# Two state updates placed earlier in an attention pipeline, and one shift of the routing moved to ScalarE

## The chip, the core and the metric

The kernel runs on one core of a Trainium2 chip. The time is the device time of one execution in microseconds (us). The engines that matter are TensorE (PE in the profile; its weight loads are PEld), VectorE (DVE), ScalarE (ACT), GpSimd (POOL) and SyncE (SP), which issues most transfers.

## What is computed

Two blocks follow each other. The first is a linear attention with a decaying state, for 4 batches, 8 heads, 768 tokens and a head width of 48; the second sends each token through one of 8 experts.

```python
for t in range(S):                       # attention, for each b, h
    cur = einsum('bhd,bhe->bhde', u * kt, vt)
    y[:, :, t] = einsum('bhd,bhde->bhe', rt, state + cur)
    state = w * state + einsum('bhd,bhe->bhde', kt, vt)
...
x = y as (B, S, H * D)                   # 4 x 768 x 384
fresh_e = argmax(x @ w_gate)             # 8 experts
e = fresh_e if s == 0 or sigmoid(x @ w_local) < 0.5 else prev_e
out = softmax(x @ w_gate)[e] * (relu(x @ w1[e]) @ w2[e])
```

The expert of a token is thus its own best one, or the one that the token before it had: a running choice along each sequence. w1 is 384x1024 for each expert, w2 1024x384.

## The kernel before

**The items.** The attention is worked off in 16 items, n = 0 to 15: a batch n // 4 and a pair of heads n % 4. Each item has 768 tokens, in 6 chunks (c) of 128. The partitions hold two heads of 48 each, at 0 and at 64. For each item the class runs these steps, each a method:

- `load`: three transfers on SP's queue: rk (r and k with the head's rows on the partitions), kv (k and v with the tokens on the partitions) and vT.
- `scale`: six products on POOL, all with both inputs in SBUF: rw, r times powers of the decay (L229, two halves); ke, k times the decay to the end of its chunk (L212, two halves); pd, r times k (L216, two halves). Up to item 2 the order is pd, ke (with rw on VectorE), for item 4 ke, rw, pd, for the others rw, ke, pd. These products lie in buffers that serve in turn.
- `keys`: kw on VectorE (L236), k divided by the powers of the decay.
- `added`: ten matmuls on PE (L248; the profile shows each matmul of the items as two rows, or passes, each transpose as one), one for each of 5 chunks and 2 heads: what each chunk adds to the state. They write `T`, 240 columns of the PSUM tile mp. There is one T for all items.
- `states`: one scan on VectorE (L254) that reads T and writes S, the state ahead of each chunk.
- `own`: four matmuls on PE (L264) on pd and one product with vT on VectorE (L268): each token's own term. It opens the PSUM tile y.
- `scores(n, half)`: twelve matmuls (L283) on kw and rw for three chunks, into one of two PSUM tiles that serve in turn ("pair"). It returns the masking product on VectorE (am, L285), which the caller places.
- `inside`: the products of am with v (L292), 24 PE passes for an item, added into y.
- `before`: the products of S with rw (L305), added into y, then ACT's copy of y to xT (L309).
- `turn`: six transposes (L318) into a "pair" tile and ACT's copies to x (L320); with a batch's last item, x goes to DRAM.

With a whole batch done, `logits` (L331) multiplies xT by the gate weights and `token_logits` turns the result, so that VectorE has each token's 9 logits.

**The order.** Each engine works through its own instructions in the order in which `run` (L341 to L479) issues them; a semaphore wait stops the engine and all that is queued behind. Iteration n of the loop holds, for most n: turn(n-2), added(n), states(n), scale(n+1), inside(n-1), before(n-1), scores(n+1) with the first half's mask at once and the second half's mask kept (`keep`), own(n), keys(n+2), keep(). Up to n = 2 the item's own added and states close the iteration. At n = 3 the scores are those of item 3 itself (`ahead`, L438), and the order behind them is own(3), added(3), keep(), states(3). At n = 4 the scores of 4 and of 5 follow each other.

**The routing in between.** E is 8 experts. The tokens' experts are found in two groups of two batches each. The steps of the first group are laid into iterations 9 to 15 of the attention (g is 8):

- n = 9 (g+1): `experts_of`: VectorE finds each token's largest logit (L671), compares (L672), weights (L673) and, in a second part at the iteration's end, forms a key (L675 to L678).
- n = 10 (g+2): behind own(10), `router.keys` turns the keys on PE into the tile mp (L684), columns that T partly shares, and `router.runs` makes the running maximum on VectorE (L689).
- n = 11 (g+3): `turn_runs` turns it back on PE (L694) into columns of mp beyond T, `last` (L701) spreads the last column, and `one_hot` (L707 to L714) yields each token's expert `ei[:, 1]` and its one-hot form oh (L712). L714, the last of it, shifts the expert number left by 9 as an integer: the number times 512, the base of the expert's slots.
- n = 12 (g+4): `counts` (L721, L722) and `ranks` (L728 to L737). n = 13: `slots`, whose L774 adds the shifted number to a token's rank. n = 14, 15: `columns`, `numbers`, `places`.

The second group does the same once, after the attention (from about 112 us), among the experts' first matmuls. From there to the end, PE works through the experts' layers.

mp is one PSUM tile of 512 columns for T, the turned keys, the turned runs and, in the first iterations, the powers of the decay (written by L157 and its like, for items 0 to 3). What writes it waits until what was there has been read.

Of the kernel before, what the change touches and what calls it, by code (L numbers as in the profile page):

```python
# [11 lines left out]
F32 = mybir.dt.float32  # L12
I32 = mybir.dt.int32
Act = mybir.ActivationFunctionType
Alu = mybir.AluOpType
# [5 lines left out]
P = 128  # L21
# [5 lines left out]
E, F = 8, 1024  # L27
# [5 lines left out]
ST = 4  # L33
# [22 lines left out]
def spread(ap, axis, n):  # L56

    a = ap.unsqueeze(axis)
    return a.to_broadcast([n if i == axis else s for i, s in enumerate(a.shape)])


class Attention:
# [278 lines left out]
    def run(self, router, fetch, heads):  # L341


        def pair(name):
            t = self.banks(name)
            return [t[:, 0], t[:, 1]]

        M = B * HP

        mp, mp_end = router.mp, 2 * P + 2 + (NCH - 1) * DH  # L350

        g = GROUPS[0][1] * HP
        for n in range(M + 1):
            if n + AHEAD - 1 < M:
                self.load(n + AHEAD - 1)
            elif n + 2 == M:
                fetch()
            if n == 0:
                self.scale(0)
                self.keys(0)  # L360
                self.tables()
                self.scores(0, 0)()
                self.scores(0, 1)()
                self.own(0)
                self.nc.scalar.copy(self.first, self.tab[:, 1, 0])
                self.turn_ends(slice(1, HP))
                self.warm(3)
                self.added(0)
                self.reciprocals(1)
                self.states(0)  # L370
                self.scale(1)
                continue
            if n < 3:

                self.keys(n)
                self.inside(n - 1)
                self.before(n - 1)
                if n == 2:
                    self.turn(0, pair("tp"))
                self.nc.scalar.copy(self.first, self.tab[:, n + 1, 0])  # L380
                self.scores(n, 0)()
                keep = self.scores(n, 1)
                self.own(n)
                keep()
                self.added(n)
                self.states(n)
                if n == 1:
                    self.reciprocals(2)
                self.scale(n + 1)
                continue  # L390
            if n < M:
                self.turn(n - 2, pair("tp"))
                if n == 3:
                    self.reciprocals(3)
                if n < 5:
                    self.keys(n)
                if n > 3:
                    self.added(n)
                    self.states(n)
            if n == 4:  # L400
                self.keys(5)
            if n > HP and n % HP == 1:
                self.token_logits(n // HP - 1, pair("lq")[0])
            if n == g + 1:
                router.experts_of(0, (0,))
            if n == g + 5:
                router.slots(0)
                router.columns(0)
            if n == g + 6:
                router.numbers(0)  # L410
            if n == M:
                router.shares(0)
            if n + 1 < M:
                self.scale(n + 1)
            if 3 <= n < 6:
                router.constants(n - 3)
            if n == M:
                self.turn(M - 2, pair("tp"))
            self.inside(n - 1)
            if n == g + 3:  # L420

                router.turn_runs(0, mp[:, mp_end:])
            self.before(n - 1)
            if n == 6:
                router.cast()
            if n == M:
                break
            if n == g + 3:
                router.last(0, mp[:, mp_end:])
                router.one_hot(0, (0,))  # L430
            if n == g + 7:

                router.summed(0, 0)
                router.copied(0, self.nc.vector.tensor_copy)
                router.head(pair("tb")[0])
                heads()

            ahead = n if n < 5 else n + 1  # L438
            if ahead < M:
                self.scores(ahead, 0)()  # L440
                keep = self.scores(ahead, 1)
            if n % HP == 0:

                keep()
                self.own(n)
                self.logits(n // HP - 1, pair("lp")[0])
                if n == 4:
                    self.scores(5, 0)()
                    self.scores(5, 1)()
                    self.keys(6)  # L450
                if n == g + 4:
                    router.counts(0, [mp, mp[:, E * NC // 2:]])
                    router.ranks(0, (0,))
                if n > 4:
                    self.keys(n + 2)
                if n == g + 4:
                    router.ranks(0, (1,))
            else:
                self.own(n)
                if n == g + 2:  # L460
                    router.keys(0, mp)
                    router.runs(0)
                if n == 3:
                    self.added(3)
                if 4 < n < M - 2:
                    self.keys(n + 2)
                if ahead < M:
                    keep()
                if n == 3:
                    self.states(3)  # L470
            if n == g + 1:
                router.experts_of(0, (1,))
            if n == g + 3:
                router.one_hot(0, (1,))
            if n == g + 5:
                router.places(0, 0)
            if n == g + 6:
                router.places(0, 1)
        self.inner.close()  # L479
# [81 lines left out]
class Router:  # L561
# [27 lines left out]
    def open(self, i, pool):  # L589
        g, c = self.g[i], self.g[i]["nc"]  # L590
        for name, shape, dt in (
                ("mx", [P, c], F32), ("eq", [P, c, E], F32), ("k", [P, c], F32), ("key", [P, c], F32),
                ("run", [c, P], F32), ("rn", [P, c], F32), ("inc", [P, c + 1], F32),
                ("ei", [P, 3, c], I32), ("oh", [P, E, c], F32),
                ("exc", [P, E, c + 1], F32), ("pos", [P, E, c], F32), ("far", [P, EARLY, c], F32),
                ("r", [P, c], F32), ("si", [P, 3, c], I32),
                ("eqv", [P, c, E * ST], F32), ("val", [P, c, E * ST], F32), ("ohq", [P, c, P], F32),
                ("ex", [P, c, E], F32), ("sm", [P, c], F32), ("pe", [P, c], F32)):
            if name != "far" or i == 0:
                g[name] = pool.tile(shape, dt, name=f"{name}{i}")  # L600
# [102 lines left out]
    def one_hot(self, i, parts=(0, 1)):  # L703

        nc, g = self.nc, self.g[i]
        if 0 in parts:
            nc.vector.memset(g["inc"][:, 0:1], 0.0)  # L707
            nc.vector.tensor_tensor_scan(g["inc"][:, 1:], g["bc"], self.go, 0.0, Alu.max, Alu.mult)
            nc.vector.tensor_tensor(g["ei"][:, 0], g["inc"][:, :g["nc"]], g["rn"], op=Alu.max)
            nc.vector.tensor_scalar(g["ei"][:, 1], g["ei"][:, 0], E - 1, None, Alu.bitwise_and)  # L710
        if 1 in parts:
            nc.vector.tensor_tensor(g["oh"], spread(g["ei"][:, 1], 1, E), spread(self.ie, 2, g["nc"]), op=Alu.is_equal)  # L712

            nc.vector.tensor_scalar(g["ei"][:, 2], g["ei"][:, 1], 9, None, Alu.arith_shift_left)  # L714

    def counts(self, i, bank):

# [52 lines left out]
    def slots(self, i):  # L770

        nc, g = self.nc, self.g[i]
        nc.vector.tensor_reduce(g["r"], g["pos"].rearrange("p e c -> p c e"), axis=AX.X, op=Alu.add)
        nc.vector.scalar_tensor_tensor(g["si"][:, 0], g["r"], float(ST * P - 1), g["ei"][:, 2], Alu.min, Alu.add)  # L774
        nc.vector.tensor_scalar(g["si"][:, 1], g["si"][:, 0], P - 1, None, Alu.bitwise_and)
        nc.vector.tensor_scalar(g["si"][:, 2], g["si"][:, 0], 7, None, Alu.arith_shift_right)

# [34 lines left out]
    def heads(self, table, out):  # L812
        self.nc.vector.tensor_reduce(out, table[:, :EARLY, :2], axis=AX.X, op=Alu.add)
# [80 lines left out]
def route(tc, once, ps, lt, ident, gates):  # L894
# [57 lines left out]
    nc.vector.tensor_copy(ccol, cp[:NC, :1])  # L952
    run = tl("run", [NC, P])
    nc.vector.tensor_tensor_scan(run, rows, rows, ccol, Alu.max, Alu.max)
    rp = bank("rp")
    nc.tensor.transpose(rp[:, :NC], run, ident[:NC, :NC])
    ei = tl("ei", [P, NC], I32)
    nc.vector.tensor_copy(ei, rp[:, :NC])
# [756 lines left out]
```

## Time and profile before

| | |
|---|---|
| time, median of 3 runs | 384.11 us (383.83 to 384.48) |
| time of the profiled execution | 385.54 us |
| its span in the trace | 383.8 us |
| granted TensorE clock | 0.996 |
| PE busy | 366.4 us, 95% of the span |
| PEld busy | 322.5 us, 84% |
| DVE busy | 251.6 us, 66% |
| POOL busy | 150.7 us, 39% |
| ACT busy | 106.5 us, 28% |

The span runs from the first to the last recorded instruction; the time of the same execution is 1.7 us longer. The shares are means over the whole span; the kernel has stages with different limits, and the attention ends at about 112 us, so the shares of its stretches have to be read by themselves:

| stretch, us | length | PE | DVE | POOL | DMA share |
|---|---|---|---|---|---|
| 0 to 27 | 27 | 24.01 | 21.68 | 20.56 | 0.93 |
| 27 to 36 | 9 | 7.33 | 6.84 | 8.60 | 1.02 |
| 36 to 66 | 30 | 29.59 | 23.47 | 30.00 | 0.98 |
| 66 to 80 | 14 | 12.49 | 12.87 | 12.59 | 1.00 |
| 80 to 112 | 32 | 29.18 | 24.91 | 15.07 | 0.51 |
| 112 to 384 | 272 | 263.79 | 161.78 | 63.83 | 0.41 |

Each number under an engine is its busy time in us in that stretch. A line of the timeline below gives the start, the length, the engine, the source line, the operation and its output and inputs with their sizes; "x20" means 20 instructions of the same kind in one row, and a square bracket at the end the idle time ahead and what ended it.

### The profile page before, as it was taken

Reading aid. Unit: us, or ns where it says so; the run is one execution under the profiler, and the core shown is the slowest. Engines: PE = TensorE matmul, PEld = TensorE weight load, DVE = VectorE, ACT = ScalarE, POOL = GpSimd, SP = SyncE. Lnnn points to the kernel's source line nnn. Section 1 sums busy time; section 2 is a strip of 40 time slices with the busy share of each in tenths; the row PEclk is TensorE's granted clock in tenths of the full one; section 3 lists DMA queues with packets and bytes.
Section 4 is the critical chain, followed back from the end, with each engine's and each line's share of the span. In section 5 each row is a group of like instructions: output and inputs, shape, how many; then the busy total and the mean of one; then the engine's idle time right before and its main releaser. Section 6 shows DMA issues by size and latency. Waiting matters only on the chain. (4 is left out here: it accounts for less than half of the span.)

```text
span 383.8 us, 9675 instructions
## 1 busy us (share of the span) xinstructions
PE 366.4 (95%) x3846; PEld 322.5 (84%) x3846; DVE 251.6 (66%) x722; ACT 106.5 (28%) x288; POOL 150.7 (39%) x212
## 2 busy tenths in 40 slices
PE   7998999898999999999999999999999999999992
PEld 6775777676759998999999999999989899899971
DVE  6888778978935745587556757658758758456400
ACT  4131232222222111322323233234234233232220
POOL 8689999877222041411432313213313113012022
PEclk9999999999999999999999999999999999999998
DMA  7999998989115880830561165145246146064011
GB/s 255 410 411 409 407 387 305 372 303 393 55 32 200 321 351 13 288 151 23 205 205 64 42 189 209 54 172 206 76 165 227 38 172 233 10 213 171 3 37 36
DMA packets 17478, 74.97 MB, mean 195 GB/s; under 512 B 2730, under 2 KB 6587, under 8 KB 14865
## 3 DMA queue, kind: packets, MB, share of 16 engines
q1 hardware_dynamic: 10048, 56.89, 39.4%
q0 software_dynamic: 3424, 9.52, 7.6%
q10 hardware_dynamic: 3952, 7.87, 5.6%
q8 instruction: 32, 0.52, 0.6%
q14 instruction: 22, 0.17, 0.1%
HBM read 64.83 MB, written 9.51 MB: 194 GB/s over the span
## 5 line engine op out<-in xcount | busy, mean ns | idle before, releaser
L1272 POOL DMA_INDIRECT out_dram<-yo,sid x27 | 26.7, 988 | 102.4 <-ACT yo L1267 79.0
L1123 PE MATMUL h<-exT,w1t 128*128 128x168 f32 (+4 forms) x240 | 54.9, 327 | 0.0
L1127 DVE TENSOR_TENSOR hT<-h,hs 128x168 f32<-128x168 f32 (+3 forms) x60 | 21.0, 351 | 46.6 <-PE h L1123 31.0
L1046 POOL DMA_INDIRECT xg<-x_d,gid x29 | 31.2, 1075 | 37.7 <-DVE sm L881 17.4
L1123 PEld LDWEIGHTS h<-exT,w1t 128*128 128x128 f32 x240 | 41.7, 190 | 0.3 <-issue 0.3
L1073 PE MATMUL h<-exT,w1t 128*128 128x192 f32 (+1 forms) x192 | 38.3, 338 | 0.0
L1192 PE MATMUL y<-factors,sums 128*128 128x192 f32 x168 | 36.8, 326 | 0.0
L1123 PE MATMUL h<-xs,ws 128*128 128x168 f32 (+4 forms) x144 | 35.2, 326 | 0.0
L216 POOL TENSOR_TENSOR pd<-rk 128x384 f32<-128x384 f32 x32 | 31.4, 1003 | 9.3 <-PE y L264 7.1
L285 DVE TENSOR_TENSOR am<-pair,kept 128x768 f32<-128x768 f32 x32 | 30.0, 950 | 7.2 <-PE pair L283 6.6
L1073 PEld LDWEIGHTS h<-exT,w1t 128*128 128x128 f32 x192 | 32.3, 190 | 1.5 <-issue 0.2
L1123 PEld LDWEIGHTS h<-xs,ws 128*128 128x128 f32 x144 | 25.5, 190 | 4.3 <-ACT hs L1130 1.2
L1192 PEld LDWEIGHTS y<-factors,sums 128*128 128x128 f32 x168 | 28.9, 190 | 0.0
L292 PE MATMUL y<-am,kv 128*64 128x128 f32 x384 | 25.1, 276 | 1.1 <-DVE y L268 1.1
L212 POOL TENSOR_TENSOR ke<-kv,endT 128x288 f32<-128x288 f32 x32 | 24.9, 799 | 2.5 <-DMA kv<-in_kv_dram 1.7
L283 PE MATMUL pair<-rw,kw 48*64 48x128 f32 (+1 forms) x768 | 22.9, 249 | 1.4 <-ACT end L167 0.6
L229 POOL TENSOR_TENSOR rw<-rk,tab 128x384 f32<-128x384 f32 x26 | 23.7, 930 | 1.2 <-DMA rk<-in_rk_dram 1.2
L309 ACT COPY xT<-y 128x768 f32<-128x768 f32 (+1 forms) x16 | 12.5, 780 | 40.0 <-PE y L305 40.0
L292 PEld LDWEIGHTS y<-am,kv 128*64 128x64 f32 x384 | 21.1, 137 | 2.6 <-DVE y L268 1.6
L1192 PE MATMUL y<-w2t,hT 128*128 128x192 f32 x96 | 23.0, 328 | 0.0
L1060 DVE COPY exT<-tp 128x384 f32<-128x384 f32 (+6 forms) x29 | 14.0, 488 | 13.8 <-PE tp L1059 13.6
L283 PEld LDWEIGHTS pair<-rw,kw 48*64 48x64 f32 x768 | 19.4, 133 | 3.7 <-issue 1.8
(279 smaller groups left out, 732.8 us busy)
## 6 DMA issues: line engine op xcount, KB each, us to landing
w1t<-in_w_dram SPq DMA_DIRECT2D x9, 1536.0 KB, 6.7
w2t<-in_w_dram SPq DMA_DIRECT2D x9, 1536.0 KB, 7.6
rk<-in_rk_dram SPq DMA_DIRECT2D x15, 768.0 KB, 9.2
kv<-in_kv_dram SPq DMA_DIRECT2D x16, 584.0 KB, 6.9
vT<-in_vT_dram SPq DMA_DIRECT2D x16, 384.0 KB, 10.0
x_d<-x ACTq DMA_DIRECT2D x4, 1152.0 KB, 10.3
w1t<-in_w_dram ACTq DMA_DIRECT2D x1, 1536.0 KB
w2t<-in_w_dram ACTq DMA_DIRECT2D x1, 1536.0 KB
```

The lines of the kernel that those rows point to most:

```text
L212: nc.gpsimd.tensor_mul(t["ke"][:, p::2], t["k"][:, p::2], spread(self.endT[:, p, hp], 1, C2))
L216: nc.gpsimd.tensor_mul(t["pd"][:, z], t["rT"][:, z], t["kT"][:, z])
L229: engine.tensor_mul(t["rw"][:, z], t["rT"][:, z], spread(pw, 1, z.stop - z.start))
L283: nc.tensor.matmul(sc[f * DP:(f + 1) * DP, h, i, x:], lhsT=t["kw"][q, c, o * DP:(o + 1) * DP], rhs=t["rw"][q, c, x:], start=True, stop=True)
L285: return lambda: nc.vector.tensor_mul(t["am"][:, g], sc, spread(self.kept[:, g:g + 3], 1, 2))
L292: nc.tensor.matmul(t["y"][p * DP:(p + 1) * DP, h, c2 * P:(c2 + 1) * P], lhsT=t["v"][:, (2 * c + h) * DH:(2 * c + h) * DH + DP], rhs=t["am" ...
L1046: self.nc.gpsimd.indirect_dma_start(out=xg[:n], out_offset=None, in_=self.x_d[:rows], in_offset=bass.IndirectOffsetOnAxis(ap=u["gid"][:n, ...
L1073: nc.tensor.matmul(h[:, :n], lhsT=u["w1"][:, m, kk, :], rhs=u["xT"][:, kk, :], start=(kk == 0), stop=(kk == DK - 1))
L1123: nc.tensor.matmul(out, lhsT=a, rhs=b, start=start and k == 0, stop=stop and k == len(terms) - 1, skip_group_check=True)
L1127: nc.vector.tensor_tensor(out, a, b, op=Alu.add)
L1192: return lambda: nc.tensor.matmul(bank[:, x * half:(x + 1) * half], lhsT=a, rhs=b, start=(j == 0 and x == 0), stop=(j == FK // 2 - 1), ski ...
L1272: self.nc.gpsimd.indirect_dma_start(out=out.rearrange("n (h d) -> (n h) d", h=2) if half else out, out_offset=bass.IndirectOffsetOnAxis(ap ...
```

## The change

It has three parts.

A. At n = 3, added(3) and states(3) are issued ahead of scores(3). Before, added(3) stood behind own(3), and states(3) behind the second mask.

B. added(11) is issued in iteration 10, between own(10) and `router.keys`. Before, it stood at the start of iteration 11, behind turn(9). states(11) stays where it was.

C. The shift L714 leaves VectorE. In its place ACT writes the expert number times 512 as a float into a tile of its own, eb, with one ACTIVATE (Copy, scale 512). L774 reads eb. This holds for both groups, so it concerns two instructions in all.

```diff
@@ run
                 if n > 3:
-                    self.added(n)
+                    if n != g + 3:
+                        self.added(n)
                     self.states(n)
...
             ahead = n if n < 5 else n + 1
+            if n == 3:
+                self.added(3)
+                self.states(3)
             if ahead < M:
                 self.scores(ahead, 0)()
                 keep = self.scores(ahead, 1)
...
                 self.own(n)
                 if n == g + 2:
+                    self.added(n + 1)
                     router.keys(0, mp)
                     router.runs(0)
-                if n == 3:
-                    self.added(3)
                 if 4 < n < M - 2:
                     self.keys(n + 2)
                 if ahead < M:
                     keep()
-                if n == 3:
-                    self.states(3)
@@ open
-                ("ei", [P, 3, c], I32), ("oh", [P, E, c], F32),
+                ("ei", [P, 2, c], I32), ("eb", [P, c], F32), ("oh", [P, E, c], F32),
@@ one_hot
             nc.vector.tensor_tensor(g["oh"], spread(g["ei"][:, 1], 1, E), spread(self.ie, 2, g["nc"]), op=Alu.is_equal)
-            nc.vector.tensor_scalar(g["ei"][:, 2], g["ei"][:, 1], 9, None, Alu.arith_shift_left)
+            nc.scalar.activation(g["eb"], g["ei"][:, 1], Act.Copy, scale=float(ST * P))
@@ slots
-        nc.vector.scalar_tensor_tensor(g["si"][:, 0], g["r"], float(ST * P - 1), g["ei"][:, 2], Alu.min, Alu.add)
+        nc.vector.scalar_tensor_tensor(g["si"][:, 0], g["r"], float(ST * P - 1), g["eb"], Alu.min, Alu.add)
```

The order in which the engines receive their instructions changes as the diff says and nowhere else: PE has the same matmuls, with a row of ten moved in two places, VectorE has one scan moved and two instructions fewer, ACT has two more, POOL and SP have the same in the same order.

## The prediction, made before the changed kernel was run

> Items are counted from 0, as in the code: the title's items 4 and 12 are n = 3 and n = 11. "am(4,0)" is the masked score of item 4's first half (L285).
>
> **What bounds the kernel now.** The chain of waits ends in an output DMA and says nothing of the middle, so I read the windows by stage first: in 36 to 66 us PE is busy 29.59 of 30 us, after 112 us 263.79 of 272. But in 27 to 36 us it is busy 7.33 of 9, in 66 to 80 12.49 of 14. PE is the bound with two leaks, and the change sits in both. POOL (30.00 of 30) and the DMA (share 0.98) are full in 36 to 66 too, so each must be shown not to be the next bound. Then the timeline of the first leak:
>
> ```profile
> 28.37 0.96 DVE L285 TENSOR_TENSOR am<-pair,kept 128x768 f32<-128x768 f32 x1 [0.84 <-PE pair L283]
> 29.34 0.66 PE L248 MATMUL mp<-kv,ke 128*48 128x48 f32 x20
> 29.92 0.80 PE L318 MATMUL pair<-ident,xT 112*128 112x112 f32 x6
> 30.39 0.95 DVE L285 TENSOR_TENSOR am<-pair,kept 128x768 f32<-128x768 f32 x1
> 31.26 0.64 DVE L254 TENSOR_TENSOR_SCAN S<-step,mp 128x240 f32<-128x240 f32 x1
> 32.00 0.66 PE L248 MATMUL mp<-kv,ke 128*48 128x48 f32 x20 [1.28 <-issue]
> 32.46 1.53 PE L292 MATMUL y<-am,kv 128*64 128x128 f32 x24
> 33.91 0.79 PE L305 MATMUL y<-rw,S 48*48 48x128 f32 x18
> ```
>
> [...]PE idles 1.28 us before added(4) at 32.00. The page calls it "issue", but scan(3), which still reads T, ends at 31.90, and added(4) overwrites T: that is the wait. Second leak:
>
> ```profile
> 65.98 2.40 DVE L672 TENSOR_TENSOR eq<-lt,mx 128x96 f32<-128x96 f32 x1
> 66.71 1.55 POOL L212 TENSOR_TENSOR ke<-kv,endT 128x288 f32<-128x288 f32 x2
> 69.40 1.97 POOL L216 TENSOR_TENSOR pd<-rk 128x384 f32<-128x384 f32 x2 [1.14 <-PE y L264]
> 69.60 0.79 PE L318 MATMUL pair<-ident,xT 112*128 112x112 f32 x6 [0.37 <-DVE am L285]
> 75.56 0.79 PE L318 MATMUL pair<-ident,xT 112*128 112x112 f32 x6 [0.45 <-DVE am L285]
> 76.79 0.66 PE L248 MATMUL mp<-kv,ke 128*48 128x48 f32 x20 [0.44 <-issue]
> 78.33 0.63 DVE L254 TENSOR_TENSOR_SCAN S<-step,mp 128x240 f32<-128x240 f32 x1
> 79.02 0.23 PE L694 MATMUL mp<-ident,run 12*128 12x12 f32 x1 [0.25 <-DVE inc L707]
> 85.86 0.98 DVE L714 TENSOR_SCALAR ei<-ei 128x12 int32<-128x12 int32 x1
> 88.30 1.50 PE L331 MATMUL pair<-xT,wp 128*32 128x384 f32 x16 [0.31 <-DVE am L285]
> ```
>
> From 65.30 to 79 DVE runs without a gap, and PE waits for it at 69.60, 75.56 and 79.02. The wait at 76.79 is for the run scan L689 (76.29, 0.40 long), which reads the same tile mp.
>
> [...]L714 takes 978 ns beside POOL's L229 and 167 ns later, when POOL is idle; L672 2399 against 258 ns. Inputs from PSUM (L285, L268, L236, L254) show no such stretch. [...]Seven VectorE instructions met that here: L676, L677, L712, L714, L729, L737 got through at the end of the POOL instruction then running; L672 let two such ends pass (66.74, 67.50) and finished only when POOL stopped at 68.26 because pd(11) waited for own(9). [...]the trace's ACT CAST L662 of 128x8 took 200 ns. The built order adds no table load.
>
> **Part A, item 3.** No work is added or removed; 20 passes (0.66 us) and a scan (0.64 us) move. Added(3) goes behind before(2), whose last weights are loaded by 26.92 (L305 at 26.24, 0.68 long). Its inputs are there: ke(3) since 24.82, the last write of mp before it (L157) at 26.39. It issues to 27.45 and ends at about 27.58. PE idled then anyway: 0.39 us until kw(3) at 27.50, so scores(3), queued behind it, starts as before. Cover gone: 0.1 us at most. Scan(3) runs 27.65 to 28.30 in VectorE's 0.84 us gap before am(3,0) at 28.37. Then:
> - PE: turn(2) follows own(3), at 29.40 (am(3,0) must end, 29.33), not 29.92. Added(4) needs scan(3) (28.30) and ke(4) (28.95): 29.98, not 32.00.
> - Inside(3) then needs L268(3) (ends 30.49) for its first 10 passes and am(3,1) (ends 31.34) for the other 14. What is late next is am(3,1). From 31.40, 14 passes at 0.85 us (the same 14 at 18.39) end at 32.25; with the usual 0.17 us before(3) starts at 32.42, not 33.91: 1.49 us earlier.
> - VectorE: kw(4) from 31.26, scan(4), kw(5) to 33.64; am(4,0) is wanted at 33.82. It holds by 0.2 us.
>
> Is it kept? POOL has no gap from 27.40 to 68.26, so its times don't move; PE's margins to it are own(4) 3.0 us (35.80 against pd(4) 32.79), scores(5) 3.2, scores(6) 3.1, scores(7) 3.4, scores(8) 3.2, scores(9) 3.4. All exceed 1.5. Loads: rk(6), issued at 23.05 and at most 11 us in flight, lands by 34.4 and is wanted at 39; the gap grows afterwards. So A brings **-1.5 us** by iteration 8. ACT's copies follow PE.
>
> **Iteration 9, touched by no edit.** L672 is issued at 64.49 instead of 65.98, and own(9) ends at 67.75 instead of 69.23. So pd(11) finds no wait at 68.22 and POOL's gap goes. L672's cost is unknown: at the best it is granted at the next end, 65.09; at the worst only at POOL's next gap. I take the first (six cases of seven): L672 ends at 65.2, L673 at 66.05, both before scores(10,0) at 66.44; am(10,0) ends at 67.39 and turn(8) follows own(9) directly at 67.66. The 0.37 us of idle PE at 69.60 is regained: **-0.3**. L676 and L677 meet POOL again as before (71.3, 72.2), and the VectorE chain to scan(11) keeps -1.8. A lost end costs about 0.8 us: -1.0 in all.
>
> **Part B, added(11).** Ten matmuls (0.66 us) go from 76.79 to behind own(10). Its wait is scan(10) (ends 74.65); ke(11) is there since 68.26. Behind it queue router.keys and turn(9): keys ends about 0.55 later, 75.65, yet VectorE comes to L689 only at 76.29; turn(9) waits for am(11,0), 75.51, anyway. Inside(10) starts at about 76.44 (L268(10)), not 77.21. But L694 behind it still waits for scan(11), and scan(11) was held by VectorE's queue (L285 to 78.41), not by added(11) (77.45). PE just waits longer at L694. **0**; at the best 0.44 + 0.25 = -0.7, if VectorE's chain shortens; at the worst +0.1.
>
> **Part C.** VectorE loses L714 twice (0.98, 0.17), ACT gains two of 0.2. In iteration 11 ACT has ei from 81.10 and is idle from 80.92 to 83.47: free. In the second group ei is ready at 124.89 and the next ReLU wants ACT at 125.36: free, its cover 0.27 us. Scan(12) and am(13,0) move up 0.7, and PE's 0.31 us before L331 goes. Then L729 is asked at 90.41 instead of 90.72, both under POOL's L229 (90.22 to about 91.07), and added(13) behind it starts as before. **0**; at the best -0.3.
>
> No instruction of SP or POOL is moved. Sum: -1.5 - 0.3 = -1.8. Against the profiled execution: span 383.8 to 382.0, time 385.54 to 383.7 (1.7 us around the span). That execution is 1.4 above the median, 384.11, for which the same step gives **382.3**.
>
> **The rivals.**
> - L672 holds out until POOL's old gap time, 68.26, as before: VectorE then starts its long run at the same instant, A is eaten, 384.1 (with C at its best 383.8). For: it has passed ends before. Against: six of seven.
> - Slower: [...]The point of decision is 68.22: A has closed the gap that let it through. POOL goes on with pd(11) and rw(12) to 72.1 and stops only because ke(12) needs added(10), which stands behind turn(8), am(10,0) and L672. Then am(10,0) ends at 73.4 and turn(8) comes at 73.45 instead of 69.59, +3.9; some 0.7 comes back where L676 and L677 then find POOL idle: +3.2, 387.3. For: this very instruction held out through two ends. Against: ends of the same kinds (L229 to L212, L212 to L212) were won by others.
> - B and C pay in full: 1.8 + 0.7 + 0.3 = 2.8, 381.3.[...]
> - The change moving nothing: excluded; the built order shows the moved rows.
>
> **How the numbers follow.** Forecast (one lost end included, 381.8 to 383.2) 0.66; gain eaten 0.11; starved 0.15; full pay 0.08. What a measurement of this kernel tells from no change is about 0.2%, 0.77 us. Faster: 0.66 + 0.08 less 0.01 = 0.73; same 0.11; slower 0.16. The range, 381.2 to 384.6, takes in all but the starved case and the tails.
>
> **What would show it.** Right: L248 of item 4 at about 30.0 without idle before it; L305 of item 3 near 32.4; L672 below 0.8 us; L694 still waiting for scan(11); L714 gone from VectorE and an ACT row of about 0.2 us. Wrong: am(3,0) later than 28.5; PE waiting for POOL between 36 and 66; L672 of several us with POOL never idle around it; ReLUs at 125 late.

## The result and the profile after

The changed kernel takes 383.41 us (median of 22 runs, 382.38 to 384.82), the kernel before on the same occasion 384.30 us (22 runs). The ratio is 0.9972, 95% interval 0.9962 to 0.9982: 1.1 us faster (0.7 to 1.5). 382.3 had been forecast, with a range of 381.2 to 384.6.

The profiled execution took 383.35 us, with a span of 381.6 us. That is 2.2 us less than the span of before, twice what the timings say. The reason is in the experts' part: from own(15)'s product (L268) to the end, the traces of this study fall in two groups, 274.7 us (nine traces, the kernel before in both of its own) and 273.8 us (five). The five are the changed kernel and the four of the last occasion; on these two occasions the kernel before had medians of 384.3 and 384.2, on the two others 385.1 and 385.4. The groups differ at one place, some 36 us behind own(15), where PE waits for a ReLU on ScalarE in the nine and not in the five. These 0.9 us go with the occasion and not with the edit: kernels with all three parts stand in both groups. What held ScalarE there is not known, and no trace of the kernel before falls in the second group, so that for this kernel it is read from the medians alone. What is left of the 2.2 is 1.26 us at own(15), 107.88 against 109.14.

The windows of the changed kernel (busy us and instructions of PE, PEld, DVE, ACT, POOL, then clock, DMA share, GB/s) for the two leaks:

```profile
27.00:36.00 9.00, 8.76 (x208) 6.58 (x210) 7.63 (x11) 2.30 (x4) 8.53 (x13) 1.00 1.02 411
66.00:80.00 14.00, 12.36 (x286) 9.71 (x282) 12.52 (x17) 3.39 (x8) 12.58 (x15) 1.00 0.97 351
```

PE is busy 8.76 us in the first, not 7.33: that leak is mended. In the second it is busy 12.36, not 12.49: that one is as wide as it was. The first leak in the timeline of the changed kernel (PE and DVE; start, length, engine, line):

```profile
26.98 0.65 PE L248 MATMUL mp<-kv,ke 128*48 128x48 f32 x20
27.68 0.65 DVE L254 TENSOR_TENSOR_SCAN S<-step,mp 128x240 f32<-128x240 f32 x1 [0.25 <-PE mp L248]
28.41 0.96 DVE L285 TENSOR_TENSOR am<-pair,kept 128x768 f32<-128x768 f32 x1
29.47 0.80 PE L318 MATMUL pair<-ident,xT 112*128 112x112 f32 x6
30.07 0.97 DVE L268 TENSOR_TENSOR y<-y,vT 128x768 f32<-128x768 f32 x1 [0.69 <-PE y L264]
30.19 0.66 PE L248 MATMUL mp<-kv,ke 128*48 128x48 f32 x20
31.09 1.94 PE L292 MATMUL y<-am,kv 128*64 128x128 f32 x24 [0.24 <-DVE y L268]
32.96 0.79 PE L305 MATMUL y<-rw,S 48*48 48x128 f32 x18
```

Added(3) and scan(3) lie where they should, and added(4) starts at 30.19 with no wait (before: 32.00). But before(3) starts at 32.96, not at the 32.42 of the forecast: L268 of item 3 begins at 30.07 instead of 29.52, and everything behind it on VectorE with it. The second leak:

```profile
65.65 2.75 DVE L673 TENSOR_TENSOR eq<-lt,mx 128x96 f32<-128x96 f32 x1
66.75 1.54 POOL L212 TENSOR_TENSOR ke<-kv,endT 128x288 f32<-128x288 f32 x2
68.62 0.95 DVE L285 TENSOR_TENSOR am<-pair,kept 128x768 f32<-128x768 f32 x1
69.07 1.96 POOL L216 TENSOR_TENSOR pd<-rk 128x384 f32<-128x384 f32 x2 [0.78 <-PE y L264]
69.63 0.79 PE L318 MATMUL pair<-ident,xT 112*128 112x112 f32 x6 [0.73 <-DVE am L285]
74.86 0.66 PE L248 MATMUL mp<-kv,ke 128*48 128x48 f32 x20
77.98 0.63 DVE L254 TENSOR_TENSOR_SCAN S<-step,mp 128x240 f32<-128x240 f32 x1
78.67 0.23 PE L695 MATMUL mp<-ident,run 12*128 12x12 f32 x1 [0.91 <-DVE inc L708]
80.79 0.21 ACT L715 ACTIVATE eb<-ei 128x12 f32<-128x12 int32 x1 [0.21 <-DVE ei L711]
```

The compare (L672 before, L673 here) is asked for 0.33 us earlier and takes 0.35 us longer; am(10,0) starts at 68.62, before at 68.59. PE waits for it 0.73 us, before 0.37: what is left of part A's lead has become a wait in front of turn(8). POOL keeps it, however: its pd(11) starts at 69.07, before at 69.40. Added(11) is at 74.86 as part B wants it, and PE stands 0.91 us in front of the turned runs. The ScalarE product of part C takes 0.21 us.

Here is the lead over the kernel before at L268, by item, from the starts of this line in the traces:

| item | 3 | 4 | 5 | 6 | 7, 8 | 9 | 10 | 11 | 12 | 13 to 15 |
|---|---|---|---|---|---|---|---|---|---|---|
| changed kernel, us | -0.55 | 0.80 | 0.66 | 0.61 | 0.33 | -0.03 | 0.35 | 0.85 | 1.42 | 1.26 |
| second trace of before (run 8) | 0.00 | 0.00 | 0.00 | 0.28 | 0.28 | 0.27 | 0.28 | 0.78 | 0.80 | 0.85 |

The second line was taken later and matters much: of the 1.26 us, 0.85 lie between two executions of the same kernel. The first line has three parts.

- 0.35 us at item 10. It is PE's lead at own(9) (68.02 against 68.35), handed on by POOL: pd(11) waits for own(9), so POOL's next instructions end some 0.35 us earlier, and with them the key step, which ends within 0.1 us of a POOL instruction in both (first the kernel before, then the changed kernel). In eight of the ten traces with the compare in SBUF, item 10's product comes 5.96 to 6.03 us behind the start of pd(11).

```profile
72.33 1.01 DVE L676 TENSOR_TENSOR k<-t,k 128x12 f32<-128x12 f32 x1
72.36 0.63 DVE L677 TENSOR_TENSOR k<-t,k 128x12 f32<-128x12 f32 x1
```

- 0.50 us at item 11. It goes with a stop of PE in scores(12) (0.43 us, in the table of run 7) that the first trace of the kernel before has and its second has not.
- 0.41 us between items 11 and 13 (run 6).

Against the second trace the changed kernel leads by 0.06 us at item 10 and by 0.41 us at items 13 to 15.

### The profile page after: what moved, and what is told of

The parts are those of the page before. It is cut to its first block, busy times and chain, and to the rows that moved or that the text cites. A ratio compares the mean times of both kernels' runs of the same rounds, so it can differ in the third digit from the quotient of the medians.

```text
span 381.6 us, 9675 instructions
## 1 busy us (share of the span) xinstructions
PE 366.2 (96%) x3846; PEld 322.8 (85%) x3846; DVE 251.4 (66%) x720; ACT 107.2 (28%) x290; POOL 150.7 (39%) x212
## 5 line engine op out<-in xcount | busy, mean ns | idle before, releaser
L285 DVE TENSOR_TENSOR am<-pair,kept 128x768 f32<-128x768 f32 x32 | 30.0, 952 | 6.2 <-PE pair L283 5.5
L229 POOL TENSOR_TENSOR rw<-rk,tab 128x384 f32<-128x384 f32 x26 | 23.6, 928 | 1.1 <-DMA rk<-in_rk_dram 1.1
L309 ACT COPY xT<-y 128x768 f32<-128x768 f32 (+1 forms) x16 | 12.5, 781 | 40.1 <-PE y L305 40.1
```

Of the source, the lines that this page charges most:

```text
L229: engine.tensor_mul(t["rw"][:, z], t["rT"][:, z], spread(pw, 1, z.stop - z.start))
L285: return lambda: nc.vector.tensor_mul(t["am"][:, g], sc, spread(self.kept[:, g:g + 3], 1, 2))
```

## The experiments

Ratios are to the kernel before on the same occasion, with 95% intervals; its medians were 385.12 us for runs 1 to 4, 385.39 for runs 5 to 8 and 384.22 for runs 9 to 12. VectorE's "borders" are explained at run 6, PE's, with its "fetches", at run 7.

**1. Part A alone.**

```diff
+            if n == 3:
+                self.added(3)
+                self.states(3)
             if ahead < M:
                 self.scores(ahead, 0)()
...
-                if n == 3:
-                    self.added(3)
...
-                if n == 3:
-                    self.states(3)
```

> Part A alone (added(3) and states(3) ahead of scores(3)), without B and C. Theory 1, from the two traces: A gives item 4 a lead of about 0.8 us, [...]and the compare L672 then holds VectorE until POOL stops near 68.3 us, so that am(10,0) starts at 68.6 as before; only POOL's earlier pd(11) is left, some 0.3 us: time ratio 0.999. Rival (the prediction's main case): A's 1.5 us stays, L672 ends before 66.4: ratio 0.995 to 0.996. Second question: is L268 of item 3 again 0.5 us later than in the kernel before (30.07 against 29.52)? If it is a matter of A's order it comes back; if of chance it does not.

384.73 us, ratio 0.9990 (0.9977 to 1.0002). Lead at L268: 0.78 at item 4, 0.62 at 5, 0.02 at 7, -0.13 at 9. L268 of item 3 is late again, at 30.10. Nothing of A is left at item 9, and almost nothing at item 7 already: PE stood 0.61 us at its border at 52 us in this trace. The prediction's main case, 0.995 to 0.996, is excluded for A alone; a gain of up to 0.9 us is not.

**2. Part B alone.**

```diff
-                    self.added(n)
+                    if n != g + 3:
+                        self.added(n)
...
                 if n == g + 2:
+                    self.added(n + 1)
                     router.keys(0, mp)
```

> Part B alone (added(11) behind own(10)). Theory 1: B does nothing at L694, which still waits for scan(11) at about 79.0, [...]own(11) comes 0.4 to 0.5 us earlier: ratio 0.999. Rival (prediction): B is worth 0; own(11)'s product stays at 82.8, ratio 1.000. Rival 2: B at its best, L694 0.7 us earlier: ratio 0.998.

384.93 us, ratio 0.9999 (0.9983 to 1.0014). The turned runs start at 79.08 (before 79.02). The stop in scores(12) is gone, but PE ran slowly from 80.4 to 84 in this trace (L264 took 1.54 us instead of 0.88), so that it says nothing of item 11. By run 8 that stop is chance, so theory 1, which set B's gain on it, falls; the value 0 of the prediction fits.

**3. Part C alone.**

```diff
-            nc.vector.tensor_scalar(g["ei"][:, 2], g["ei"][:, 1], 9, None, Alu.arith_shift_left)
+            nc.scalar.activation(g["eb"], g["ei"][:, 1], Act.Copy, scale=float(ST * P))
...
```

> Part C alone (the shift on ScalarE). Theory 1: VectorE's chain in item 12 ends 0.6 us earlier (scan(12), am(13,0), am(13,1)), since L714 took 0.98 us there under POOL; PE's wait ahead of L331 goes and the rest stays through POOL's pd(13): ratio 0.9985 (-0.6 us). Rival (prediction): given back at the scan L729, ratio 1.000, with added(13) at 91.97 as before.

384.63 us (the median of before is 385.12), ratio 1.0002 (0.9983 to 1.0021): the timing doesn't settle it. The trace does a part: from own(11) to own(13) this kernel gains 0.42 us on before, as the changed kernel does (0.41). Where these come from is shown at run 6.

**4. The compare and the keys in PSUM.** The changed kernel with

```diff
         lg = lt[:, g["z"], :E]
+        if i == 0:
+            g["eq"] = self.mp[:, 128:224].rearrange("p (c e) -> p c e", e=E)
+            g["mx"], g["k"] = self.mp[:, 224:236], self.mp[:, 236:248]
```

> The changed kernel with the first group's largest logit, its compare and its key product (mx, eq, k) kept in free columns of the PSUM tile mp instead of SBUF, so that the compare, the weighting and the two key steps have an input in PSUM. [...]it takes 0.26 us instead of 2.75, am(10,0) starts at 66.9 instead of 68.6, pd(11) no longer waits at 68.3, and the time falls by 1 to 1.5 us below the changed kernel: ratio to before 0.993 to 0.995. If the compare is slow for another reason (its three-dimensional operands, the two reads of lt), it stays above 2 us and the ratio stays 0.997.

388.08 us, ratio 1.0085 (1.0068 to 1.0103): slower. Its timeline, from the fastest of its six executions (386.27 us):

```profile
65.63 0.26 DVE L676 TENSOR_TENSOR mp<-lt,mp 128x96 f32<-128x96 f32 x1
67.65 0.96 DVE L285 TENSOR_TENSOR am<-pair,kept 128x768 f32<-128x768 f32 x1 [1.47 <-PE pair L283]
72.09 0.17 DVE L681 SCALAR_TENSOR_TENSOR key<-lt,mp 128x12 f32<-128x12 f32 x1
72.36 0.66 PE L248 MATMUL mp<-kv,ke 128*48 128x48 f32 x20 [2.78 <-POOL rw L229]
```

With one input in PSUM the same compare takes 0.26 us while POOL runs (2.75 us in the changed kernel, with both in SBUF), and am(10,0) comes 0.97 us earlier. (Its result lies in PSUM too, but that isn't the reason: the weighting of run 5, L677, has one input in PSUM and its result in SBUF, and takes 0.26 us beside POOL as well.) But added(10) now stands 2.78 us. The page names POOL; the program's own semaphore names L681, the last reader of mp, which ends at 72.26, though it reads other columns than added(10) writes. This wait, which the experiment brought with it, is longer than the 0.73 us that PE waited behind the compare in the changed kernel.

**5. Only the compare in PSUM.** The changed kernel with

```diff
-            nc.vector.tensor_tensor(g["eq"], lg, spread(g["mx"], 2, E), op=Alu.is_equal)
-            nc.vector.tensor_tensor(g["eq"], g["eq"], spread(self.down, 1, g["nc"]), op=Alu.mult)
+            nc.vector.tensor_tensor(eq, lg, spread(g["mx"], 2, E), op=Alu.is_equal)
+            nc.vector.tensor_tensor(g["eq"], eq, spread(self.down, 1, g["nc"]), op=Alu.mult)
...
```

where eq and mx of the first group are columns 128 to 235 of mp.

> The changed kernel with only the largest logit and the compare (mx and the compare's result) of the first group in free columns of the PSUM tile mp; the weighted result and the key steps go back to SBUF, so that the last reader of mp ahead of added(10) is the weighting at about 66.2 us and added(10) no longer waits for the keys (in the run before it waited 2.78 us). [...]0.26 us for it, am(10,0) at about 67.6 instead of 68.6, added(10) at about 69.5, the two key steps still stretched (0.6 to 0.7 each), scan(10) 0.4 to 0.6 earlier than in the changed kernel: ratio to before 0.9955 to 0.9965. Rival: what is gained is lost again under POOL in the key steps, ratio 0.997.

383.92 us, ratio 0.9958 (0.9945 to 0.9971).

```profile
65.91 0.26 DVE L676 TENSOR_TENSOR mp<-lt,mp 128x96 f32<-128x96 f32 x1
67.94 0.96 DVE L285 TENSOR_TENSOR am<-pair,kept 128x768 f32<-128x768 f32 x1 [1.47 <-PE pair L283]
72.35 0.89 DVE L681 SCALAR_TENSOR_TENSOR key<-lt,k 128x12 f32<-128x12 f32 x1
73.17 0.64 DVE L254 TENSOR_TENSOR_SCAN S<-step,mp 128x240 f32<-128x240 f32 x1
```

As expected in the trace: scan(10) starts at 73.17 instead of 73.66. The time is in the expected range too, but the rival's 0.997 and the changed kernel's own 0.9972 (0.9962 to 0.9982) are not excluded, so that a gain over the changed kernel isn't shown. One of the two key steps is still slow beside POOL (L681, 0.89 us; 0.17 in run 4, with an input in PSUM).

**6. One more instruction on VectorE**, in the setup, on top of run 5:

```diff
         nc.vector.memset(tab[:, 0, :, 0:1], 1.0)
+        nc.vector.memset(tab[:, 0, :, 0:1], 1.0)
```

> The kernel of the run before this one plus one tiny memset on VectorE in the setup, which writes again what is there already. In the changed kernel and in A alone L268 of item 3 is VectorE's recorded instruction 63 and starts 0.48 us after its wait has ended; in the kernel before it is number 62 and starts 0.05 us after. [...]the extra memset (L268 becomes number 64, the wait 63) takes the 0.48 us away: L268 of item 3 at 29.6 instead of 30.07, own(4)'s product at about 35.7 instead of 36.2. If the 0.48 us belongs to the order of A itself, nothing moves. On the whole time I expect little of it[...]: ratio 0.9950 to 0.9965; nothing below 0.9950 unless those stops are chance.

384.30 us, ratio 0.9974 (0.9959 to 0.9988). L268 of item 3 starts at 29.78, 0.05 us behind its wait, no longer 0.48 (29.6 had been expected, but the wait itself ended later). This shows the cause of the late L268. Counting VectorE's recorded instructions from 0, semaphore waits included, L268 of item 3 is number 62 without part A, 63 with it and 64 here; L268 of item 13 is number 191 without part C, 190 with it, and 191 again here. In all 14 traces the delay of these two instructions behind their wait is 0.48 or 0.49 us at number 63, 0.40 at number 191, and 0.04 or 0.05 at the others. A third case lies 384 further on, at number 575: in the four traces without part C it is a product of the experts' part (L1127 in the kernel before), and it starts 0.40 us behind its wait; in run 6 the same product is number 574 and starts 0.04 us behind. For item 13, first in the kernel before and then in the changed kernel, the view of line L268 shows the wait (DVEq) and the product:

```profile
L268 DVEq EVENT_SEMAPHORE  x1: 1246/1246/1246, 96.0 to 96.0; - x1
L268 DVE TENSOR_TENSOR y<-y,vT x1: 967/967/967, 97.7 to 97.7; 128x768 f32<-128x768 f32 x1
```

```profile
L268 DVEq EVENT_SEMAPHORE  x1: 1246/1246/1246, 95.1 to 95.1; - x1
L268 DVE TENSOR_TENSOR y<-y,vT x1: 967/967/967, 96.4 to 96.4; 128x768 f32<-128x768 f32 x1
```

The columns after the count are the shortest, median and longest ns, then first and last start. The wait ends at 97.25 before and at 96.35 after; the product starts 0.40 us and 0.04 us behind it. 63, 191 and 575 lie multiples of 128 apart; I call these numbers VectorE's borders. What happens at them isn't shown. Part A moved one scan and so pushed L268 of item 3 onto a border. Part C took one instruction away and pulled L268 of item 13 off one. What that is worth can be read from item 10's product to item 15's: 32.79 to 32.82 us in six traces with part C and number 190 (changed, C alone, run 4, run 7, without B, without A; 32.89 in run 5), 33.15 in run 6, which has part C and number 191, and 33.15 in A alone and in before again, which don't have part C. (The first trace of before and B alone take 33.71 and 34.62, with PE's slow stretches in scores(12) and own(11); runs 9 and 10 have another order there.) The gain of 0.35 us belongs to the border and not to the work of L714. For the kernel as a whole the forecast of 0.9950 to 0.9965 was missed: PE stops 0.54 us at 33.4 us in this trace, at one of its own borders, and most of the 0.43 us is gone at item 4 (own(4)'s product at 36.34, not 35.7).

**7. The first batch's x written later**: the 1152 KB write that the changed kernel issues at 40.5 us is issued at 57.2 us.

```diff
-        if h0 == H - 2:
+        if h0 == H - 2 and b:
...
+        if n == 6:
+            self.write(0)
...
```

> The changed kernel with the write of the first batch's x (1152 KB, issued at 40.5 us) issued two iterations later. It takes 1152 KB out of the stretch 40 to 51 us[...]. [...]the fetches for the borders at 46.2 and 51.8 start less than 3 us after the border before (3.65 and 3.37 in the changed kernel), these two stops go, and own(7)'s product keeps the lead that own(5) has (0.66), so it comes at 56.1 instead of 56.46. The stop at 40.1 lies ahead of the write and stays.[...] Later items are worse or equal, since the write then meets that of the second batch.

One execution, 385.92 us. The page has a queue "q8 instruction: 32, 0.52 MB"; the trace's transfer records give the start of each of the 32, and 16,384 bytes for each. I call them fetches. What they carry isn't shown; that they go with PE's stops is my estimate from the counts: PE has 7,810 recorded rows in the kernel before, 244 for each of the 32. Numbering these rows (matmuls, weight loads and waits together) from 0, PE's stops without a semaphore in this part of the kernel lie at numbers 193 + 256 k. I call these PE's borders. Start of the fetch that belongs to a border, counted from the border before, and PE's stop there (from the start of one matmul or weight load to the start of the next, so a little more than the idle time that a timeline gives):

| border | before | before again (run 8) | changed | run 7 |
|---|---|---|---|---|
| 1473 (40 us) | 3.5, no stop | 3.1, no stop | 3.7, 0.26 | 3.7, 0.40 |
| 1729 (46 us) | 3.6, 0.32 | 3.2, no stop | 3.7, 0.37 | 3.7, 0.26 |
| 1985 (52 us) | 2.6, no stop | 2.7, no stop | 3.4, 0.36 | 1.1, no stop |
| 2241 (57 us) | 1.8, no stop | 1.8, no stop | 2.0, no stop | 0.8, no stop |
| 2497 (62 us) | 2.1, 0.3 (rhythm) | 2.2, 0.3 (rhythm) | 2.5, no stop | 3.7, 0.8 |
| 2753 (69 us) | 1.2, no stop | 1.6, no stop | 1.5, no stop | 4.5, 1.0 |
| 3009 (74 us) | 3.2, no stop | 2.7, no stop | 3.0, no stop | 3.7, 0.75 |
| 3265 (81 us) | 5.3, 0.43 | 3.0, no stop | 3.2, no stop | 3.9, no stop |

("Rhythm": L331's passes stand 0.3 us apart anyway.) In the first trace of before and in the changed kernel, the five stops of 0.26 us and more end 2.2 to 2.5 us after the start of their fetch, and PE passes the other eleven borders 2.5 to 4.6 us after it. With the write moved the stops lie elsewhere: the one at 52 us is gone, and behind 57 us there are stops of 0.8, 1.0 and 0.75 us, at 62, 69 and 75. This rests on one trace, and the two columns of the kernel before show how much stops come and go by chance. The one at 46 us, which I had expected to go, stayed, and own(7)'s product comes at 56.48 and not at 56.1, so the x write isn't all of the load there. Run 7's timeline, with L336 for L331:

```profile
61.57 2.35 PE L336 MATMUL pair<-xT,wp 128*32 128x384 f32 x16
67.73 1.27 PE L283 MATMUL pair<-rw,kw 48*64 48x128 f32 x46
69.73 0.88 PE L264 MATMUL y<-pd,w_t 48*64 48x384 f32 x8 [0.74 <-issue]
```

L336 takes 2.35 us, where L331 took 1.50, and a wait "<-issue" stands in front of L264.

**8. The kernel before once more.**

> The kernel before, unchanged, for a second trace, to tell chance from cause. What belongs to the program should return: added(4) waiting for scan(3) until about 32.0, the compare L672 ending only at 68.2, L268 of item 13 (VectorE's instruction 191) 0.40 us behind its wait. What is chance may not: the 0.45 us stop of PE in scores(12) at 81.3, where the fetch started 5.3 us after the border before and the four other kernels show 1.6 to 3.7.

One execution, 384.63 us. What was called the program's returned (compare until 68.11, L268 of item 13 0.40 us behind its wait). The stops at 46 and 81 us did not.

**9. states(11) early**: the changed kernel with

```diff
                     if n != g + 3:
                         self.added(n)
-                    self.states(n)
+                        self.states(n)
...
                     router.runs(0)
+                    self.states(n + 1)
```

> The changed kernel with states(11) moved too: the scan runs right behind the running maximum in iteration 10, ahead of kw(12) and the second mask. The prediction held that part B is worth nothing because the turned runs still wait for scan(11), which VectorE's queue holds until 78.5 us. If so, scan(11) now ends at about 76.9, the turned runs follow inside(10) at about 77.9 without PE's 0.9 us of idle time, and everything behind comes 0.7 to 0.9 us earlier: own(11) at 81.2 instead of 82.0, ratio to before 0.9945 to 0.9960. If what follows is bound by POOL (pd(12)) or by VectorE's longer queue to am(11,1), nothing of it is left at 112 us: ratio 0.997.

382.52 us, ratio 0.9949 (0.9931 to 0.9968); the upper end reaches a little into the changed kernel's interval.

```profile
75.40 1.53 PE L292 MATMUL y<-am,kv 128*64 128x128 f32 x24
75.43 0.62 DVE L254 TENSOR_TENSOR_SCAN S<-step,mp 128x240 f32<-128x240 f32 x1
76.86 0.23 PE L696 MATMUL mp<-ident,run 12*128 12x12 f32 x1
78.56 0.86 DVE L711 TENSOR_TENSOR ei<-inc,rn 128x12 int32<-128x12 f32 x1
```

The turned runs follow inside(10) without a wait. From own(10) to own(11) the kernel takes 6.18 us, the changed kernel 6.90. A part is given back at once: L711, 0.17 us before, takes 0.86.

**10. Runs 9 and 5 together.**

> The kernel of the run before this one with the compare of the first group kept in PSUM as well. If both places are separate, the gains add: ratio to before 0.9925 to 0.9945 (0.0014 from the compare, 0.002 from the scan, on the changed kernel's 0.997). If item 13 is reached by POOL's queue first, it is no better than the better of the two alone, 0.9950 to 0.9960.

382.25 us, ratio 0.9949 (0.9933 to 0.9965): no faster than run 9. The gains don't add. In its trace PE sits idle for 0.48 us in scores(12), at the border 3265, whose fetch started 4.3 us after the border before; I can't tell whether that is the reason.

**11. A and C without B; 12. B and C without A.**

> Parts A and C without B. Prediction: B is worth 0, so the ratio is that of the changed kernel, 0.997. Rival: B [...]starts inside(10) earlier, and some 0.4 us is missing here: 0.998.

> Parts B and C without A. Theory from the traces: A's lead of 0.8 us at item 4 is gone at am(10,0) in every trace, because the compare there ends 0.1 us after POOL stops whatever the time at which VectorE asks for it; so B and C without A are as fast as all three but for the 0.3 us by which own(9) and POOL's pd(11) come earlier: ratio 0.997 to 0.998. If A's lead does pay, it is missing here: ratio 0.999 to 1.000.

Without B: 383.55 us, ratio 0.9981 (0.9968 to 0.9995). From the turned runs to own(11)'s product it takes 3.32 us, with B (changed kernel) 3.31: B isn't seen. Without A: 383.37 us, ratio 0.9964 (0.9951 to 0.9978), no slower than all three parts. If A's lead paid, 0.999 to 1.000 had been expected; that is excluded. A gain of A of a few tenths of a us can't be seen at these intervals.

The compare over all ten traces that have it in SBUF:

| kernel | asked for | ends | POOL stops |
|---|---|---|---|
| before, before again | 65.98, 65.70 | 68.38, 68.11 | 68.26, 67.99 |
| changed | 65.65 | 68.41 | 68.29 |
| A alone, B alone, C alone | 65.96, 66.04, 65.67 | 68.51, 68.39, 68.89 | 68.39, 68.28, 68.77 |
| run 7, run 9 | 66.52, 65.37 | 68.51, 67.57 | 68.39, 67.45 |
| without B, without A | 65.70, 65.87 | 68.47, 68.42 | 68.35, 68.30 |

It ends 0.12 us after POOL has stopped, in each of them, whenever it was asked for; in the changed kernel it lets three ends of POOL instructions pass (65.96, 66.78, 67.54). L712 and L737 of the kernel before, as large as the compare, end 0.12 us after an end of POOL too (85.94 and 85.82, 93.67 and 93.55), but after the first that they meet. And POOL stops 40.8 us after it begins ke(4), which varies from 26.64 to 27.95 between the traces, whichever parts a kernel has.

## Why the prediction was right or wrong

The sign was right and the number lay in the range, but mostly by luck: the range held nearly no change as well (384.1, the gain eaten), the lead that the forecast counted on came to little, and a gain that it put at nothing stood in its place.

- **Part A, "-1.5 us by iteration 8".** Wrong. Wait and order were read rightly: added(3) and scan(3) fit into the two gaps, and added(4) lost its wait. Three things were missed. L268 of item 3 came 0.55 us later, 0.44 of it by the border at 63, so that before(3) led by 0.95 and item 4's product by 0.80. "PE's margins to POOL ... all exceed 1.5" was true, but the next bound was neither POOL nor a load: PE's stops at its borders (40.1 and 51.8 us) took 0.14 us of the lead at item 5 and 0.28 at item 7. So 0.33 of the 1.5 us reached own(9). At the compare VectorE lost this too, but POOL handed it on to item 10 (0.35). How much of it is A's is open: without A, PE's lead there is 0.28 us in the second trace of before and 0.31 in C alone, and A alone has 0.02.
- **"At the best it is granted at the next end ... I take the first (six cases of seven)."** This step failed. The right case was the rival "gain eaten", with a chance of 0.11: the compare holds until POOL stops (it ends 0.12 us behind that in all ten traces). Three of the six cases that got through are as large as the compare (L712 and L737 with 96 columns, L729 with 104), so its size isn't the reason. What is remains open. The point of the slower rival was not reached: POOL stopped at 68.29 in the changed kernel too, because A's lead at own(9) was only 0.33 us by then and pd(11) still had to wait (0.78 us). The rival wasn't right in all: VectorE did not start "its long run at the same instant" with all of the lead eaten, since the key step that follows ended earlier with POOL.
- **Part B, 0.** Right, and its reason too: the turned runs waited for scan(11), held by VectorE's queue. Run 9 moves that scan, and the wait, 0.91 us in the changed kernel, is gone.
- **Part C, 0, "L729 is asked ... both under POOL's L229".** Right for the work: the lead grows by 0.57 us at item 12, and added(13) then waits 1.29 us behind L730 and L732, so the lead there (0.90) is no more than at item 11 (0.85). But some 0.4 us (0.35 from item 10 to item 15) came at item 13 from the border at instruction 191, which no step had.
- **The sum.** Forecast -1.8 (1.5 + 0.3), measured -1.1. Shown in its place: C 0.35, by the border and not by its work; of B nothing is seen, and of A no more than the 0.35 at item 10, which may be chance. Some 0.4 to 0.7 us of the 1.1 stay open. With both of these 0.35 counted, just the low end of the interval, 0.7, is reached. PE's stops can hide as much, 0.8 us at item 11 between two executions of one kernel, but that they come less often with the change isn't shown: one trace for a kernel can't tell. Runs 11 and 12 don't settle it, since their intervals overlap.

What the prediction read in L672 and L714 bears out for the compare: beside POOL it takes 0.26 us with an input in PSUM (runs 4 and 5) and 1.99 to 3.22 us with both in SBUF (the ten traces above). The four operations that the prediction names for an input in PSUM vary little over the whole trace of before: L285 925 to 959 ns, L268 948 to 967, L254 631 to 655, L236 a mean of 940 with 768 columns. What stretched L672 and L714 isn't shown. ScalarE's product, put at 0.2 us, took 213 and 214 ns.

## What to carry to other kernels

When an edit gives one engine a lead, follow the lead item by item. Here VectorE's border (0.44 us) and PE's (0.14 and 0.28 us) took most of it, and then came a VectorE operation on SBUF data that, in all ten traces, ended 0.12 us after GpSimd paused, though it was asked for 1.9 to 3.1 us ahead of the pause. With one of its inputs in PSUM it took 0.26 us beside GpSimd (runs 4 and 5); that the whole kernel gains by it isn't shown. In run 4 another reader of a shared PSUM tile became a wait of 2.78 us, so the last reader has to lie ahead of the next writer. And before a trace's difference is put down to an edit, take a second trace of the same kernel.

## What the runs showed that was not expected

- VectorE lost 0.40 to 0.49 us at its recorded instructions 63, 191 and 575, multiples of 128 apart, when it came to them idle, out of a semaphore row just ahead, so that adding or taking one tiny instruction moved up to half a microsecond elsewhere (run 6: L268 of item 3 from 0.48 to 0.05 us behind its wait). It wasn't lost after every idle time: in the changed kernel numbers 575 and 831, with no semaphore row just ahead, start 0.02 us behind the semaphore that releases them, after 0.68 and 9.47 us of idle time.
- PE stopped without a semaphore at recorded rows 256 apart. With a DMA share of 0.97 to 1.02 from 27 to 80 us, the fetch that I set against such a border starts up to 5.3 us after the border before, and PE passes the border 2.2 us after that start or later (first trace of before and changed kernel, the borders of run 7's table). The stops are 0.26 to 0.43 us long in the changed kernel and before, up to 1.0 us in run 7. Where they fall differs between two executions of one kernel.
